# Moving LayerNorm's scale onto the first head's query weights, and the last 64 columns of a feed-forward product onto the moving side

## The chip, the cores and the metric

The kernel runs on one core of a Trainium2 chip. The metric is device time in microseconds (us), the median over several executions. Most executions agree within 0.3%, which is 4 us here. Figures read from a trace are of one execution each. Engines: PE is TensorE (PEld its weight loads), DVE is VectorE, ACT is ScalarE, POOL is GpSimd, SP is SyncE, which here only issues transfers.

## The reference, cut to what matters

```python
mod = (silu(c) @ w_mod).reshape(1, 6, 1, 640)          # c: 1 x 640, w_mod: 640 x 3840
sa, ca, ga, sb, cb, gb = ...                           # its six rows: shift, scale, gate, twice
h = layernorm(x) * (1 + ca) + sa                       # x: 2048 x 640
q = h @ wq                                             # 32 heads of 128
o = softmax(q @ k_cache.T / sqrt(128)) @ v_cache       # 2048 keys per head
x = x + ga * (o @ wo)
h = layernorm(x) * (1 + cb) + sb
x = x + gb * B(h)          # B ends with: gelu(layernorm(x1) @ w3) @ w4, w3: 640 x 1728
...
```

The attention of 32 heads makes up most of the time. The change touches what comes before the first scores, and the product with w3: 1728 = 13 x 128 + 64, so its last block of columns is half empty.

## The kernel before: the parts that are touched

The kernel records operations with a priority, and a list scheduler puts each engine's operations into a fixed order. Each engine then executes its own list strictly in that order.

The start: five loads of 128 rows of `w_mod` (scale and shift columns side by side, 2560 bytes a row), ten one-column products per load, then transposed rows are scaled and shifted as they leave PSUM.

```python
for k in range(KT):                                    # KT = 5
    wm_load.append(dma("ACT" if k % 2 else "SP", ... w_mod[k*128:(k+1)*128, 0:2*D], ...))
...
for k in range(KT):
    def mcol(e, k=k):
        for j in range(2 * KT):                        # shift columns, then scale columns
            ins = e.matmul(mc[:, j:j+1], wm_ap[:, k, j*128:(j+1)*128], s_bf[:, k:k+1], ...)
P.op("DVE", ... tensor_copy(saT.ap, mc[:, 0:KT]) ...)
P.op("DVE", ... tensor_scalar_add(out=caT.ap, in0=mc[:, KT:2*KT], scalar1=1.0) ...)
...
# chunk 0 of the rows: 4 tiles transposed on PE, then per k one pass on DVE or ACT
hT[0][k] = transposed * caT[:, k] + saT[:, k]
# first query: five products, each in two halves of 256 rows
e.matmul(mm[:, 0:z-a], wq_t[...], hT_t[ch][:, kk, a:z], ...)
```

The feed-forward part, per chunk of 512 rows (four chunks):

```python
for f in range(NF):                                    # NF = 14 blocks, the last padded to 128
    for kk in range(KT):
        e.matmul(m.ap, w3_ap[:, kk, f*128:(f+1)*128], nT_ap[ch][:, kk, :], ...)   # 512 columns
    e.activation(gT_ap[:, f, :], m.ap, GELU)
```

## Time and profile before

| | before |
|---|---|
| median of three runs | 1369.59 us (1368.27 to 1372.08) |
| profiled execution | 1368.34 us |
| last `w_mod` piece landed / first exponential started | 9.09 / 13.78 us |
| first exponential of steps 4 and 5 | 46.72 / 54.89 us |
| from there to the last exponential | 1137.78 us |
| from the last exponential to the end | 174.35 us |

A step is one head with one chunk of 512 rows. Its eight exponentials of 1024 columns are the only ACT operations of that size, so the time at which a step's first one starts is an easy landmark. The last three rows cut the span into start, middle and tail. The transfer view of the first 16 us gives the rate in 40 slices of 0.4 us:

```profile
GB/s 0 0 0 0 54 86 250 387 394 410 403 426 403 397 403 391 384 397 403 406 296 284 245 127 289 260 137 152 211 190 246 116 172 261 263 212 239 3 8 13
```

While `w_mod` streams in, the rate stays near 400 GB/s.

### The profile page before, as it was taken

Reading aid. Unit: us, or ns where it says so; the run is one execution under the profiler, and the core shown is the slowest. Engines: PE = TensorE matmul, PEld = TensorE weight load, DVE = VectorE, ACT = ScalarE, POOL = GpSimd, SP = SyncE. Lnnn points to the kernel's source line nnn. Section 1 sums busy time; section 2 is a strip of 40 time slices with the busy share of each in tenths; the row PEclk is TensorE's granted clock in tenths of the full one; section 3 lists DMA queues with packets and bytes.
Section 4 is the critical chain, followed back from the end, with each engine's and each line's share of the span. In section 5 each row is a group of like instructions: output and inputs, shape, how many; then the busy total and the mean of one; then the engine's idle time right before and its main releaser. Section 6 shows DMA issues by size and latency. Waiting matters only on the chain.

```text
span 1367.0 us, 29510 instructions
## 1 busy us (share of the span) xinstructions
PE 1348.4 (99%) x12778; PEld 934.7 (68%) x13012; DVE 574.7 (42%) x1442; ACT 1102.6 (81%) x1145; POOL 111.5 (8%) x97
## 2 busy tenths in 40 slices
PE   9999999999999999999999999999999999999999
PEld 5677677677667767767776766776776676655665
DVE  5554344544332332333233233233323345798553
ACT  6998888888888888888888888888888888833222
POOL 1000000000000000000000000000233337500000
PEclk9999999999999999999999999999999999999999
DMA  9742624172415221341305121522236000431110
GB/s 217 150 86 51 118 28 80 37 134 48 108 37 94 51 47 36 55 90 28 55 13 99 34 47 35 94 51 48 55 65 140 22 16 19 113 84 47 41 40 31
DMA packets 264932, 90.38 MB, mean 66 GB/s; under 512 B 245065, under 2 KB 262410, under 8 KB 264794
## 3 DMA queue, kind: packets, MB, share of 16 engines
q1 hardware_dynamic: 260826, 84.17, 30.5%
q0 software_dynamic: 672, 2.56, 0.8%
q8 instruction: 104, 1.70, 0.5%
q10 hardware_dynamic: 3296, 1.67, 0.5%
q14 instruction: 34, 0.28, 0.1%
HBM read 41.68 MB, written 2.63 MB: 32 GB/s over the span
## 4 chain that ended last, share of the span: by engine, by line
PE 97%; issue 1%; DMA 1%; DVE 1%; ACT 0%; SPq 0%; DVEq 0%
PE f_O L825 35%; PE f_S L806 29%; PE f_M L729 10%; PE f_M L760 10%; PE f_M L1008 2%; PE f_O L989 2%; PE f_S L989 2%; PE f_S L1008 2%; PE f_S L940 1%; PE f_S L963 1%; PE f_M L963 1%; PE f_O L940 1%; DMA f_W<-in_w_mod_dram 0%; DMA f_hT<-f_xn 0%; PE f_S L760 0%
## 5 line engine op out<-in xcount | busy, mean ns | idle before, releaser
L808 ACT ACTIVATE f_PQ<-f_S 128x1024 bf16<-128x1024 f32 x1024 | 1042.0, 1023 | 136.5 <-PE f_S L806 103.9
L825 PEld LDWEIGHTS f_O<-f_KV,f_PQ 128*128 128x128 bf16 x8192 | 634.9, 98 | 261.3 <-DVE f_OO L834 0.2
L825 PE MATMUL f_O<-f_KV,f_PQ 128*128 128x129 bf16 x8192 | 796.4, 220 | 8.3
L806 PE MATMUL f_S<-f_PQ,f_KV 128*128 128x512 bf16 x1831 | 650.8, 379 | 2.6 <-ACT f_PQ L808 0.5
L768 DVE TENSOR_TENSOR f_y<-f_M,f_y 128x320 f32<-128x320 f32 x192 | 94.4, 492 | 465.6 <-PE f_M L760 465.6
L760 PE MATMUL f_M<-f_wo,f_OO 128*128 128x320 bf16 x992 | 272.9, 299 | 0.0
L806 PEld LDWEIGHTS f_S<-f_PQ,f_KV 128*128 128x128 bf16 x2048 | 191.6, 98 | 13.3 <-ACT f_PQ L808 1.7
L729 PE MATMUL f_M<-f_hT,f_wq 128*128 128x512 bf16 (+1 forms) x635 | 189.1, 378 | 1.9 <-DVE f_tmp L771 0.2
L760 PEld LDWEIGHTS f_M<-f_wo,f_OO 128*128 128x128 bf16 x992 | 96.3, 98 | 28.5
L834 DVE TENSOR_TENSOR f_OO<-f_O,f_rl 128x256 bf16<-128x256 f32 x256 | 108.4, 423 | 8.3
L538 POOL TENSOR_TENSOR f_y<-f_y,f_mod 128x640 f32<-128x640 f32 x32 | 49.1, 1542 | 735.5 <-DVE f_y L768 735.4
L733 DVE CAST f_PQ<-f_M 128x512 bf16<-128x512 f32 x127 | 87.9, 692 | 49.9 <-PE f_M L729 49.6
L729 PEld LDWEIGHTS f_M<-f_hT,f_wq 128*128 128x128 bf16 x640 | 62.5, 98 | 50.6 <-DVE f_hT L595 0.8
L832 DVE RECIPROCAL f_rl<-f_O 128x2 f32<-128x2 f32 x256 | 43.6, 170 | 65.7 <-PE f_O L825 54.8
L992 ACT ACTIVATE f_OO<-f_S 128x512 bf16<-128x512 f32 x28 | 16.7, 597 | 43.6 <-PE f_S L989 43.6
L766 DVE COPY f_y<-f_M 128x320 f32<-128x320 f32 x32 | 15.7, 492 | 57.1 <-PE f_M L760 57.1
L499 DVE BATCH_NORM_STATS2 f_small<-f_y 128x6 f32<-128x320 f32 (+1 forms) x72 | 32.3, 481 | 2.5 <-DMA f_y<-in_A_x_dram 1.5
L1008 PE MATMUL f_M<-f_KV,f_OO 128*128 128x320 bf16 x224 | 31.7, 299 | 0.0
L1008 PE MATMUL f_S<-f_KV,f_OO 128*128 128x320 bf16 (+1 forms) x224 | 31.0, 296 | 0.0
L544 ACT ACTIVATE f_xn<-f_y,f_small 128x640 bf16<-128x640 f32 x10 | 9.1, 915 | 26.3 <-DVE f_small L523 21.2
L661 DVE TENSOR_REDUCE f_small<-f_tmp 128x1 f32<-128x640 f32 x20 | 16.4, 820 | 30.1 <-ACT f_PQ L808 30.1
L1008 PEld LDWEIGHTS f_M<-f_KV,f_OO 128*128 128x128 bf16 x224 | 21.9, 98 | 8.9
(151 smaller groups left out, 523.6 us busy)
## 6 DMA issues: line engine op xcount, KB each, us to landing
f_KV<-in_A_v_cache_dram SPq DMA_DIRECT2D x28, 512.0 KB, 5.0
f_wo<-in_A_wo_dram SPq DMA_DIRECT2D x8, 640.0 KB, 4.2
f_wq<-in_A_wq_dram SPq DMA_DIRECT2D x7, 640.0 KB, 4.5
f_xin<-in_A_x_dram SPq DMA_DIRECT2D x13, 320.0 KB, 3.4
out_dram<-f_xin SPq DMA_DIRECT2D x15, 160.0 KB, 1.8
f_KV<-in_B_w_dram SPq DMA_DIRECT2D x5, 432.0 KB, 3.8
f_KV<-in_A_k_cache_dram SPq DMA_TRANSPOSE x128, 2.8
f_OO<-f_OO SPq DMA_TRANSPOSE x128, 2.5
```

The source lines that it names most:

```text
L538: P.op(eng, lambda e: e.tensor_tensor(out=out, in0=a, in1=b, op=op), COST[eng][0], rd, wr, prio, lat=300 if eng == "POOL" else None, dual= ...
L729: P.op("PE", lambda e, i=i, kk=kk, mm=mm, a=a, z=z: e.matmul(mm[:, 0:z - a], wq_t[g % 2][:, kk, hh * 128:(hh + 1) * 128], hT_t[ch][:, kk, ...
L733: P.op("DVE", lambda e: e.tensor_copy(q.ap, m.ap), 690, (m,), (q,), s * NP - 90)
L760: P.op("PE", lambda e, m=m, qt=qt, hf=hf, hh=hh: e.matmul(m[:, 0:HD], OT_ap[gs][:, qt, hh, :], wo_t[g % 2][:, hh, hf * HD:(hf + 1) * HD], ...
L768: P.op("DVE", lambda e, m=m, yt=yt: e.tensor_tensor(out=yt.ap, in0=m[:, 0:HD], in1=yt.ap, op=ALU.add), 490, (m, yt), (yt,), s * NP - 60)
L806: P.op("PE", lambda e, sp=sp, r=r, kt=kt: e.matmul(sp[:, r * QC:(r + 1) * QC], K_ap[b][:, kt * 128:(kt + 1) * 128], q.ap, start=True, stop ...
L808: x = P.op("ACT", lambda e, sp=sp, pt=pt: e.activation(pt.ap.rearrange("p k q -> p (k q)"), sp.ap, ACT.Exp, scale=SCALE), 1021, (sp,), (pt ...
L825: ins = e.matmul(o[bk][:, w * 129:w * 129 + 129], pt[:, r, qt * 128:(qt + 1) * 128], V_ap[b][:, u, 0:129], start=(u == 0 and w == 0), stop ...
L832: P.op("DVE", lambda e, ov=ov, i0=i0: e.reciprocal(rl_t[:, i0:i0 + 2].unsqueeze(2), ov[:, 0:258].rearrange("p (u d) -> p u d", u=2)[:, :, ...
L834: evac.append(P.op("DVE", lambda e, ov=ov, i0=i0, bk=bk: e.tensor_tensor(out=On_ap[gs][:, 2 * bk:2 * bk + 2, hh, :], in0=ov[:, 0:258].rear ...
L989: P.op("PE", lambda e, m=m, f=f, kk=kk: e.matmul(m.ap, w3_ap[:, kk, f * 128:(f + 1) * 128], nT_ap[ch][:, kk, :], start=(kk == 0), stop=(kk ...
L1008: P.op("PE", lambda e, f=f, mm=mm, o=o, c0=c0, c1=c1: e.matmul(mm[:, o:o + c1 - c0], gT_ap[:, f, i * 128:(i + 1) * 128], w4_ap[f][:, c0:c1 ...
```

## The change

Intent: let the scores start sooner, and let PE do less in the half-empty w3 block. It has three parts.

**The start.** The first head's query weights are multiplied by the scale (five 128x128 operations on POOL) in place of the rows. The shift's share is one column for that head, added when q leaves PSUM. So the rows can be transposed and copied before any modulation is known. `w_mod` is loaded as ten pieces, the five scale halves first; K and V loads wait for the last pieces; the V loads and the next heads' query weights move from ACT's queue to SP's; the first of the four LayerNorm tiles moves to ACT.

**w3.** The 64 columns become the moving operand, with the rows as weights: twenty products of 64 columns in place of five of 512 per chunk.

**An ordering of POOL and DVE.** A POOL operation with two tensor inputs that the scheduler's model would start before, or up to 0.4 us after, the end of such a DVE operation waits for it.

```diff
+                if e == "DVE":
+                    last_dual = o
+                elif last_dual is not None and s < port["DVE"] + 400.0:
+                    o.deps.setdefault(last_dual, False)
...
-    for k in range(KT):
-        wm_load.append(dma(... w_mod[k * 128:(k + 1) * 128, 0:2 * D] ..., 320, ...))
+    load_wm(wms, D, -300)          # five loads of the scale half, 1280 bytes a row
+    load_wm(wmb, 0, -297)          # then five of the shift half
...
+            A_(... activation(xn[0].ap, x.ap, ACT.Copy, scale=-1.0 / D, accum_out=mu.ap) ...)
+            A_(... activation(xn[0].ap, x.ap, ACT.Square, bias=mu.ap, accum_out=ss.ap) ...)
...
+            for k in (0, 2, 1, 4, 3):
+                P.op("POOL", ... tensor_scalar(out=xn_t[4][:, k*128:(k+1)*128], in0=wq_t[0][:, k, 0:128],
+                                               scalar1=caT[:, k:k+1], ... op0=ALU.mult), 300, ...)
...
-    load_k(0, -297.5, gate=(wm[2],))
+    load_k(0, -296.5, gate=(wmb[4],))
...
+                    ins = e.matmul(bq_ps.ap, wq_t[0][:, kk, 0:128], b_bf[:, kk:kk + 1], ...)
+            x = P.op("DVE", ... tensor_scalar_add(out=q[:, 0:QC // 2], in0=m[:, 0:QC // 2], scalar1=bq.ap) ...)
...
+        for kk in range(KT):
+            for i in range(4):
+                ... e.matmul(m[:, c0:c0 + FL], nT_ap[ch][:, kk, i*128:(i+1)*128], w3_ap[:, kk, FN*128:FF], ...)
...
```

## The prediction

> **What bounds the kernel now.** I read the page first, then the chain of waits, then the timeline of the first 16 us and of the last 145 us, since the change touches only these two stretches (and, lightly, GpSimd's start times between them).
>
> ```profile
> span 1367.0 us, 29510 instructions
> ...
> PE 1348.4 (99%) x12778; PEld 934.7 (68%) x13012; DVE 574.7 (42%) x1442; ACT 1102.6 (81%) x1145; POOL 111.5 (8%) x97
> ...
> PE 97%; issue 1%; DMA 1%; DVE 1%; ACT 0%; SPq 0%; DVEq 0%
> ```
>
> PE is busy in 1348.4 of 1367.0 us, and 97% of the chain that ended last is PE. So there are two ways to gain: let PE do less, or let its real work start sooner. Work taken from DVE, ACT or POOL elsewhere is worth nothing. A busy PE is not all useful: before the attention starts it runs filler matmuls. The timeline of the start (columns: start us, us, then engine, line, operation, tiles) shows what the first useful work waits for:
>
> ```profile
> 4.73 1.68 PE L440 MATMUL f_S<-f_ones 128*128 128x512 bf16 x7
> ...
> 8.12 0.81 PEld L465 LDWEIGHTS f_M<-f_s_bf,f_W 128*128 128x128 bf16 x22
> ...
> 8.76 1.46 DVE L531 TENSOR_SCALAR f_xn<-f_xin,f_small 128x640 bf16<-128x640 bf16 x4
> ...
> 10.55 0.54 DVE L595 TENSOR_SCALAR f_hT<-f_O,f_small 128x512 bf16<-128x512 bf16 x1 [0.19 <-PE f_O L586]
> 10.60 0.78 ACT L590 ACTIVATE f_hT<-f_O,f_small 128x512 bf16<-128x512 bf16 x1 [1.29 <-PE f_O L586]
> ...
> 13.37 0.81 PE L806 MATMUL f_S<-f_PQ,f_KV 128*128 128x512 bf16 x3 [0.27 <-ACT f_PQ L737]
> 13.78 2.86 ACT L808 ACTIVATE f_PQ<-f_S 128x1024 bf16<-128x1024 f32 x3 [0.70 <-PE f_S L806]
> ```
>
> The scores start only at 13.37 us. The chain (start, us, what) gives the reason:
>
> ```profile
> 2.61 6.49 DMA f_W<-in_w_mod_dram
> 9.14 0.40 PE f_M L465 x10
> ...
> 10.55 1.01 DVE f_hT L595 x2
> ...
> 13.37 0.39 PE f_S L806
> ...
> 34.27 4.54 DMA f_hT<-f_xn
> 38.84 1.07 DVE f_hT L602 x3
> ```
>
> The last of five w_mod transfers lands at 9.10 us, then come its ten column products, the remaining transposes, the modulation of the rows (five passes on DVE and ACT), the query projection, its eviction. The last two lines matter for a rival: there is a second start-up wait at 38.8 us, for the second chunk's rows.
>
> In the tail, PE is full too (19.95 us of 20 from 1310 to 1330 us), and the w3 products run at an even pace, ACT idle between them:
>
> ```profile
> 1225.79 1.24 PE L989 MATMUL f_O<-f_wq,f_KV 128*128 128x512 bf16 x5
> ...
> 1226.87 1.24 PE L989 MATMUL f_S<-f_wq,f_KV 128*128 128x512 bf16 x5
> 1227.07 0.60 ACT L992 ACTIVATE f_OO<-f_O 128x512 bf16<-128x512 f32 x1 [0.48 <-PE f_O L989]
> ```
>
> Each group of five starts 1.08 us after the one before: 216 ns per matmul. There are 14 groups per chunk, 4 chunks, and the fourteenth is half zeros (1728 = 13 x 128 + 64).
>
> **What the Trainium skill says.** (1) "TensorE: Matmul & The Clock Gate", section "Wait — 56ns, not 53.3ns?": warm matmuls start N/2.4 + about 2.5 ns apart, and never closer than about 25 ns. The trace agrees: 216 ns at 512 columns. (2) The same page, "Back-to-back issue gap", says a stream of weight load and matmul pairs takes about 81 ns per pair at 128 columns. Here the trace disagrees: the chain shows twelve 129-column products in 0.68 us, 57 ns each with a weight load each, so the measurement decides. (3) "ScalarE: Activation LUTs", section "What ACT_TABLE_LOAD costs": an ACTIVATE with immediates takes 186 ns + 0.833 ns per element, each pointer operand adds about 93 ns; for 640 elements and two pointers that is 905 ns, and the trace has 915. (4) "DMA: Bandwidth & Descriptors", section "Anatomy of one DMA": about 2 us of a transfer is fixed. The smallest landing time of the row transposes here is 2.6 us, which fits with a little data time.
>
> **The change, part by part.**
>
> *w3's last block.* Per chunk, five 512-column matmuls (5 x 216 = 1.08 us) become twenty with 64 moving columns, one per token tile and k, with the rows as the stationary operand. By (1) the array time is 64/2.4 + 2.5 = 29 ns, but each has its own weight load. The closest thing in the trace is the one-column products of the start: 22 loads in 0.81 us, 37 ns each. At 129 columns the load is hidden under 57 ns. My estimate for 64 columns is 37 to 42 ns, so 20 x 40 = 0.80 us. Gain 0.28 us per chunk, 1.1 us for four (1.3 us at 37 ns). The GELU of this block halves (0.60 to about 0.4 us), on an engine that waits for PE anyway: 0. One extra row transpose per chunk (2.6 to 6 us to land) is issued first in the chunk and needed 13 groups = 14 us later: 0. The w4 products keep count and size: 224 + 224 + 14 of 128 rows, as the stacked half blocks still need one full-height product per tile. The DVE and POOL fills of the pads go or change place, off the path: 0.
>
> *The start.* Rows are transposed unmodulated; the first head's weight columns are scaled instead (five 128x128 operations on POOL), and the shift comes in as five one-column products whose result is added at the eviction of q. What this takes out from behind the last w_mod transfer: ten column products become five (0.2 us less); the twenty transposes, of which now most precede it; the modulating evictions (10.55 to about 12.05 us), now plain copies of halves that start as soon as the tiles are ready. What is left behind it is, in PE order: five column products 0.2, two fillers 0.43, five 256-column query products 0.55, five one-column products 0.19, five more query products 0.55, about 0.2 of latency, the eviction with bias about 0.45, 0.25 to the first scores: 2.8 us. Today it takes 13.37 - 9.10 = 4.27 us. The total bytes ahead are the same 1.6 MB of w_mod, now in ten pieces, with the K loads held back until the second half lands; I take 9.1 us as unchanged. The first scores then start at about 11.9 us, 1.45 us sooner. Check on DVE: today its four tiles' work ends at 10.22 us; one tile less saves two statistics, one aggregate and one normalisation, 2 x 0.42 + 0.12 + 0.36 = 1.3 us, so it ends near 9.0, the second halves are copied by about 10.7, and that just meets the PE order. ACT takes the first tile: two accumulating passes of about 0.75, three small ones of 0.2 and one of 0.91, about 3 us after its table load, done near 8 us. It fits.
>
> *What comes back.* K's pieces 1 to 3 of the first head wait for the last w_mod piece, behind one V and one wq load, so the first of them goes out near 10.0 us and lands 3.3 to 4.3 us later, 13.3 to 14.3. It is needed in slot 2, now 14.86, then 13.4 us. I charge 0.35 us. The second V half goes out near 14 us and is needed near 18.2 with 5.4 us typical landing: it too may cost; I put the two together at 0.5 us. Rows of chunk 0 are modulated after the first query on DVE, 5 x 0.4 us, before the second head's projection; DVE was idle 3.56 us there, so 0. The second chunk's rows (the wait at 38.8 us, some 0.7 us of PE idle time: score pairs 38.50 to 40.29 apart where the step before has 1.11) come earlier by some 1 us, not the full 1.45, since the transposing queue is busy without much slack: another 0.2. Net of the start: 1.45 - 0.7, about 0.8 us, 1.4 if none of this bites.
>
> *GpSimd's new waits for DVE's two-input operations.* POOL is busy 111.5 us and is not on the chain: 0.
>
> Sum: 1.1 + 0.8 = 1.9 us; upper end 1.3 + 1.4 = 2.7.
>
> **The rivals.** A: transfers take the place of the waits removed, so the start gains nothing (for: the DMA share is above 0.9 from 5 us on; the wait at 38.8 us ends at a transfer and absorbs any earlier start whose transfer does not move). Then only 1.1 us, 1368.1. B: the 64-column products pace like their weight loads and array time in series (37 + 29 = 66 ns): 1.3 us per chunk, a loss of 0.2 each, and with the full start gain the total is still 0 to -0.5 us: 1369. Against it: 57 ns at 129 columns shows that load and product overlap. C: everything lands, PE order meets no wait, and the products take 33 ns: 1.7 + 1.5, or a little more if the stall at 38.8 us also shrinks: 3.5 us, 1365.6. D: ACT becomes the start's bound, because its table load now comes after more transfer issues and the first tile's chain of six operations is serial; the first tile's transposes then hold PE's order up and the scores start near 12.7: half of the start's gain gone.
>
> **Range and chances.** The medians before are 1369.59 (1368.27 to 1372.08), and the profiled run took 1368.34, so the noise of a median is some 1 us and the true level perhaps 1369. From 1369 I take 2.2 us (between the sum of 1.9 and its upper end): 1366.8 us. Range 1364.6 to 1369.2: C with a fast draw, A or B with a slow one. A 2% change would be 27 us, more than the whole start and all w3 blocks affected together; the chance of either side is under 1%.
>
> **What will show it.** Right: first scores near 11.9 us, filler and column products before it; in the tail, a run of twenty 128x64 products of about 0.8 us at the head of each w3 chunk and the span from first w3 product to the end shorter by 1.1 us; PE's instruction count up by some 60 in that line. Wrong: first scores after 12.7 us, PE idle at slots 2 to 6 before a K or V transfer, a longer gap near 38 us, or twenty products in 1.08 us or more.

## More of the kernel before

The experiments fell on three chips, so versions are compared by their difference from the kernel before that ran beside them.

The busy time in two stretches (columns: stretch, its length, busy us and instruction count of PE, PEld, DVE, ACT, POOL, then PE's granted clock, the transfer share, GB/s):

```profile
10.00:15.00 5.00, 4.42 (x33) 2.16 (x32) 2.23 (x7) 3.05 (x5) 0.96 (x1) 1.00 1.55 197
...
44.00:49.00 5.00, 4.95 (x56) 3.58 (x55) 3.16 (x10) 4.74 (x5) 0.00 (x0) 1.00 0.07 24
```

The clock is full in both, and by 44 us PE has no gaps.

## The result, and the profile after

| | before | after |
|---|---|---|
| median (four runs each, same chip) | 1369.22 us (1368.27 to 1372.08) | 1370.39 us (1368.49 to 1372.13) |
| last `w_mod` piece landed | 9.09 us | 11.18 us |
| first exponential of step 0 | 13.78 us | 16.18 us |
| first exponential of steps 4 / 5 | 46.72 / 54.89 us | 53.48 / 61.65 us |
| from step 5 to the last exponential | 1137.78 us | 1137.50 us |
| from the last exponential to the end | 174.35 us | 171.66 us |

The ratio is 1.0005 (95% interval 0.9982 to 1.0028): the same at the 2% limit, but not the gain of 2 us that was predicted, and outside the range given. A ratio is the mean time of one kernel's fast runs over that of the other's of the same rounds, so it is not quite the ratio of the medians quoted here. The rows of the table already locate everything: the tail gained 2.7 us, the start lost 6.8 us in this execution (the profiled one, 1372.13 us, the slowest of the four).

The page of the changed kernel looks just like that of the kernel before:

```profile
span 1370.8 us, 29671 instructions
...
PE 1349.5 (98%) x12844; PEld 937.1 (68%) x13078; DVE 574.8 (42%) x1446; ACT 1105.4 (81%) x1155; POOL 114.8 (8%) x102
...
PE 97%; DMA 1%; issue 1%; ACT 1%; DVE 0%; SPq 0%; DVEq 0%
```

PE still makes 97% of the chain. Its busy time seems to have risen (1348.4 us before), but both traces lack 234 of PE's records; in the two repetitions of experiment 1, whose traces hold all of them, it fell from 1361.9 to 1360.3 us. Averages over the span hardly show this change; the stages do. The timeline of the start (start us, us, engine, line, operation, tiles; in brackets the idle time and what ended it):

```profile
9.38 0.16 DVE L488 TENSOR_SCALAR f_small<-f_M 128x5 f32<-128x5 f32 x1 [1.03 <-PE f_M L479]
...
9.96 3.06 POOL L643 TENSOR_SCALAR f_xn<-f_wq,f_small 128x128 bf16<-128x128 bf16 x5 [8.09 <-DMA f_wq<-in_A_wq_dram]
...
10.29 0.72 PE L479 MATMUL f_M<-f_s_bf,f_W 128*128 128x1 bf16 x15 [0.15 <-DMA f_W<-in_w_mod_dram]
10.38 0.43 DVE L548 TENSOR_SCALAR f_xn<-f_xin,f_small 128x640 bf16<-128x640 bf16 x1
...
12.99 1.27 PE L774 MATMUL f_M<-f_hT,f_xn 128*128 128x256 bf16 x5
...
15.77 0.81 PE L860 MATMUL f_S<-f_PQ,f_KV 128*128 128x512 bf16 x3 [0.36 <-ACT f_PQ L790]
16.18 2.85 ACT L862 ACTIVATE f_PQ<-f_S 128x1024 bf16<-128x1024 f32 x3 [0.70 <-PE f_S L860]
```

Four things are to be seen. The scale columns are ready at 9.5 us, ahead of the shift columns. The five weight scalings on POOL take 3.06 us and can start only when the weights have landed. PE waits for shift columns that land later than all of `w_mod` did before. And the last LayerNorm tile is normalised only at 10.38 us. The chain of waits (start, us, what) holds the second loss:

```profile
3.56 6.68 DMA f_W<-in_w_mod_dram
...
36.87 7.04 DMA f_hT<-f_xn
...
45.05 0.61 PE f_M L774
```

The wait for the second chunk's rows, which ended at 38.8 us before, ends at 43.9 us now. Transfer rate and clock of the same stretches as before:

```profile
GB/s 0 0 0 0 32 125 250 394 387 390 378 349 320 263 221 317 330 373 339 311 304 338 350 325 254 134 57 20 1 172 156 45 137 205 271 252 86 133 99 179
```

```profile
10.00:15.00 5.00, 4.81 (x56) 3.56 (x54) 2.42 (x11) 1.32 (x4) 4.01 (x6) 0.66 0.68 130
...
44.00:49.00 5.00, 4.24 (x20) 2.06 (x22) 3.59 (x11) 1.26 (x2) 0.00 (x0) 0.66 0.87 274
```

The rate sags between 4.4 and 6.4 us, down to 221 GB/s, and the granted clock is 0.66 in both stretches: in each there is a window of 3.41 us at half clock (from 10.92 and from 45.05 us). The Trainium skill, "TensorE: Matmul & The Clock Gate", section "What's actually happening", says that PE runs at half clock after an idle window of about 3.4 us (3413 ns) and that the windows are not tied to the program. The trace agrees in length and in factor, but the stretches before were not idle: PE was busy for 2.54 of the 3.42 us before the first window and for 1.28 of the 3.41 us before the second. The halving explains part of why the same kernel's executions differ: of the nine of the changed kernel, the three with a mean clock of 0.998 or 0.999 took 1370.9 to 1372.1 us, and of the six at full clock five took 1368.0 to 1370.0 us and one 1371.88. The kernel before has such executions too, only fewer (of the 17 on experiment 1's chip, one at 0.998 took 1371.33 us and one at 0.999 took 1373.15).

In the tail, the new products (the timeline again, of the first chunk's w3 part):

```profile
1231.19 0.75 PE L1044 MATMUL f_O<-f_KV,f_wq 128*128 128x64 bf16 x20
1231.99 2.10 PE L1052 MATMUL f_S<-f_wq,f_KV 128*128 128x512 bf16 x9
```

A trap lies here. The next group begins 0.80 us after these twenty, which would be exactly the predicted time. But in the trace's records the twenty start 29 ns apart, 19 x 29 = 0.55 us from first to last, and the next recorded start comes 0.246 us after the last. That is 29 + 217 ns: the record of one 512-column product is missing (the trace holds 63 of the 65 products of this part). So twenty take 20 x 29 = 0.58 us. The repetition's trace (`a1_again` below), which holds all records, shows it directly:

```profile
1228.04 0.75 PE L1044 MATMUL f_O<-f_KV,f_wq 128*128 128x64 bf16 x20
1228.62 2.32 PE L1052 MATMUL f_S<-f_wq,f_KV 128*128 128x512 bf16 x10
```

A check that needs no single record: from the last exponential to the start of the last w4 block is 155.76 us before and 153.77 after, 1.99 us less, which is four times 1.08 - 0.58. The tail as a whole is 2.7 us shorter; the other 0.7 us lies behind that point and is not explained (in the other versions with the w3 part the tail is 171.6 to 172.3 us).

### The profile page after: what moved, and what is told of

It is laid out like the page before. It is cut to its first block, busy times and chain, and to the rows that moved or that the text cites. A ratio compares the mean times of both kernels' runs of the same rounds, so it can differ in the third digit from the quotient of the medians.

```text
span 1370.8 us, 29671 instructions
## 1 busy us (share of the span) xinstructions
PE 1349.5 (98%) x12844; PEld 937.1 (68%) x13078; DVE 574.8 (42%) x1446; ACT 1105.4 (81%) x1155; POOL 114.8 (8%) x102
## 4 chain that ended last, share of the span: by engine, by line
PE 97%; DMA 1%; issue 1%; ACT 1%; DVE 0%; SPq 0%; DVEq 0%
PE f_O L879 35%; PE f_S L860 29%; PE f_M L774 10%; PE f_M L814 10%; PE f_M L1071 2%; PE f_S L1071 2%; PE f_S L1052 2%; PE f_O L1052 2%; PE f_S L1016 1%; PE f_S L993 1%; PE f_O L993 1%; PE f_M L1016 1%; DMA f_hT<-f_xn 1%; DMA f_W<-in_w_mod_dram 0%; ACT f_PQ L862 0%
## 5 line engine op out<-in xcount | busy, mean ns | idle before, releaser
L774 PE MATMUL f_M<-f_hT,f_wq 128*128 128x512 bf16 x630 | 188.5, 380 | 3.9 <-DVE f_hT L578 2.0
L1071 PEld LDWEIGHTS f_S<-f_KV,f_OO 128*128 128x128 bf16 x224 | 21.7, 98 | 8.2
```

The costliest lines, as they stand in the source:

```text
L774: P.op("PE", lambda e, i=i, kk=kk, mm=mm, a=a, z=z, w=w: e.matmul(mm[:, 0:z - a], w, hT_t[ch][:, kk, a:z], start=(i == 0), stop=(i == KT - ...
L1071: P.op("PE", lambda e, f=f, mm=mm, o=o, c0=c0, c1=c1: e.matmul(mm[:, o:o + c1 - c0], gT_ap[:, f, (i % 2 if f == FN else i) * 128:][:, 0:12 ...
```

## The experiments

**Theory.** The w3 part gains 2 us, and the start loses more than that, for four separable reasons: the smaller pieces of `w_mod` move slower; POOL's scaling sits on the path; K's held-back loads push the transposing queue, and with it the second chunk's rows; and the order within DVE and PE. **Rivals.** The w3 part does not gain and the difference is merely noise; or one cause (the clock halving, or shift columns behind the last piece) makes up the whole loss; or the POOL-DVE ordering costs time.

### 1. Both kernels again

No edit. Repetitions of the changed kernel (first) and of the kernel before (second).

> The changed kernel once more. Theory (the start loses what the w3 blocks gain): the profile again has its first exp after 14.5 us (16.18 before this run, 13.78 in the kernel before), and from the last exp to the end it is about 2 us shorter than the kernel before (171.7 against 174.4). Rival (the one profile caught a bad draw of the transfers, the start is neutral): first exp at 13.5 us or sooner and the median about 2 us below the kernel before.

> The kernel before against itself, for the noise: ratio 1.000 within 0.002. Theory: first exp within 0.5 us of 13.78 and step 5's first exp within 1 us of 54.89. Rival (the start's transfers differ this much from run to run): either of them off by 2 us or more.

Measured: 1370.04 us (1367.99 to 1371.65), ratio 1.0005 [0.9992, 1.0018]; and 1368.53 us, ratio 0.9998. So the changed kernel is some 1.2 us slower or equal, certainly not 2 us faster. Its new trace, at full clock from 6.8 us on, where the record of the clock begins, still starts at 16.05 us, and step 5 at 58.50 us; the kernel before has 14.19 and 55.37 us in its new trace, within what was expected of it.

A second way to count helps from here on. Counted from the landing of the last `w_mod` piece, the first exponential follows after 4.63 to 4.78 us in all six traces with the old start, after 5.00 us in the profiled execution of the changed kernel, part of which ran at half clock, and after 4.00 us in this repetition (16.05 - 12.05). So the path behind the landing did become shorter, by 0.7 us; the landing, 3.0 us later than in the kernel before's first trace, makes up more than the whole loss at the first exponential here. Timeline lines of the repetition:

```profile
10.84 2.99 POOL L643 TENSOR_SCALAR f_xn<-f_wq,f_small 128x128 bf16<-128x128 bf16 x5 [8.97 <-DMA f_wq<-in_A_wq_dram]
...
13.89 0.28 PE L774 MATMUL f_M<-f_hT,f_xn 128*128 128x256 bf16 x1 [0.22 <-POOL f_xn L643]
...
17.79 0.59 PE L860 MATMUL f_S<-f_PQ,f_KV 128*128 128x512 bf16 x2 [0.91 <-DMA f_KV<-in_A_k_cache_dram]
```

The fifth query product waits for POOL, and the scores of the second slot wait 0.91 us for a K piece. Both waits are there without any clock halving, so the halving cannot be the whole cause.

### 2. The parts alone: w3, the start, the ordering

w3 alone is the kernel before with the w3 and w4 edits only; the start alone is the changed kernel with these undone (it keeps the ordering).

```diff
 # w3 alone: before.py
+        m = Tile(pool="T")
+        for kk in range(KT):
+            for i in range(4):
+                ... 128x64 products ...
-        for f in range(NF):
+        for f in range(FN):
 ...
 # start alone: the changed kernel with this reversed
```

> The kernel before with only the w3 and w4 part of the change (last block as twenty 64-column products, layout, pads). Theory: the start is that of the kernel before (first exp 13.8 us), each 20 products take 0.6 us, not 1.08, so the time is 1.9 us less, ratio 0.9986. Rival (the w3 part gains nothing in the end, the 2 us seen in the trace are jitter of the last transfers): ratio 1.000, last exp to end 174 us.

> The kernel before with all of the change but its w3 and w4 part. Theory: first exp 14.5 to 16.5 us, step 5's first exp 2 to 7 us later than before's 54.89, the time 2 to 5 us longer, ratio 1.002 to 1.0035. Rival (start neutral or a gain as predicted): first exp under 13.5 us, ratio 0.999 to 1.000.

Measured: w3 alone 1367.31 us (1366.88 to 1367.92), ratio 0.9985 [0.9972, 0.9998]; start alone 1372.95 us (1372.55 to 1376.79), ratio 1.0031 [1.0017, 1.0046]. One part gains and the other loses, and the intervals of both exclude 1. But w3 alone is not as good as its tail promises: its tail is 172.00 us (174.35 before), while its middle is 1138.81 us, 1.03 us longer than before, although no operation of the middle changed. Its trace shows where, in the second to last step:

```profile
1175.91 1.55 POOL L542 TENSOR_TENSOR f_hT<-f_tmp,f_y 128x640 bf16<-128x640 f32 x1
...
1176.24 3.39 DVE L865 SCALAR_TENSOR_TENSOR f_y<-f_hT,f_small,f_mod 128x640 f32<-128x640 bf16 x1
...
1177.42 1.53 POOL L542 TENSOR_TENSOR f_y<-f_y,f_mod 128x640 f32<-128x640 f32 x1
...
1180.09 1.25 PE L733 MATMUL f_M<-f_hT,f_wq 128*128 128x512 bf16 x5 [0.89 <-DVE f_tmp L775]
```

A DVE operation with two tensor inputs that elsewhere takes 0.87 us took 3.39 us: it lay under two POOL operations with two inputs each, ended 0.68 us after the second of them, and PE waited 0.89 us for what came behind it on DVE. (In the kernel before the same operation took 1.88 us: the collision was there in a mild form.) The Trainium skill, "GPSIMD Engine Reference", section "Specifications", says that POOL's memory interfaces are shared with DVE and that DVE instructions with two inputs contend; this trace agrees, with a factor of nearly 4. So the ordering, which the prediction put at 0, was tried: once with w3, once alone.

```diff
 # w3 and ordering: w3 alone, and
+                if e == "DVE":
+                    last_dual = o
+                elif last_dual is not None and s < port["DVE"] + 400.0:
+                    o.deps.setdefault(last_dual, False)
 # ordering alone: before.py with these lines only
```

> The kernel before with the w3 and w4 part and the part that keeps GpSimd's shared-port operations behind DVE's, that is the change without anything of its start. The last attention step took 10.2 us with the w3 part alone, 9.1 in both the kernel before and the changed one. Theory G (the GpSimd part removes this 1.1 us): the last step takes 9.1 us, the time is 1366.1 us, ratio 0.9977. Rival (the 1.1 us are an accident of the order, GpSimd's part does nothing): 1367.2, ratio 0.9985.

> The version with the w3 part and GpSimd's waits and the old start, once more on this chip beside the other two: 1365.5 to 1366.8 us again, ratio 0.9975 to 0.9985; if the earlier gain was the luck of one chip, 1367 or more.

> The kernel before with GpSimd's new waits for VectorE's two-input operations alone. Theory 1 (the waits only repair a collision in the last attention step that the w3 part brings, as that step took 9.14 us in the kernel before already): same as the kernel before within 0.5 us, 1368.3 to 1369.2. Theory 2 (the two engines hold each other up elsewhere too): 1366.9 to 1367.8, about 1.3 us faster, with the difference spread over several steps of the attention. My prediction's figure of 0 holds under theory 1.

Measured: w3 and ordering 1365.96 us (1365.40 to 1366.57), ratio 0.9978 [0.9965, 0.9992], and again 1366.31 us, ratio 0.9980 [0.9967, 0.9994]. Ordering alone 1368.73 us, ratio 0.9997. In the trace of the two together:

```profile
1176.77 0.87 DVE L871 SCALAR_TENSOR_TENSOR f_y<-f_hT,f_small,f_mod 128x640 f32<-128x640 bf16 x1
...
1177.72 1.54 POOL L548 TENSOR_TENSOR f_hT<-f_tmp,f_y 128x640 bf16<-128x640 f32 x1 [1.23 <-DVE f_y L871]
```

POOL now waits 1.23 us for DVE, DVE is done in 0.87 us, and the middle is 1137.50 us. The ordering has almost no gain of its own (0.23 us of the middle's length, nothing in the median); it repairs a collision that the w3 part's shifted schedule makes worse, and is worth about 1 us with it: 1.30 us of the middle in the traces (1138.80 - 1137.50), and 0.8 to 1.2 us of the medians (-1.6 us for w3 alone, -2.4 and -2.8 us with the ordering, each against the kernel before of its own chip). This is the first of two places where two parts of the change cannot be added up singly. The version with w3 and the ordering, on the old start, beats both kernels.

The sums close: start part +4.0 us (1372.95 - 1368.92), w3 with ordering -2.4 and -2.8 us (against 1368.67 and 1368.76), together +1.2 to +1.6; the changed kernel's repetition measured +1.1.

### 3. Whole rows of `w_mod`

```diff
-    load_wm(wms, D, -300)
-    load_wm(wmb, 0, -297)
+    for k in range(KT):
+        dma(... w_mod[k * 128:(k + 1) * 128, 0:2 * D] ..., 320, (), (wms[k], wmb[k]), -300 + 0.1 * k)
```

> The changed kernel with w_mod loaded again in five pieces of whole 2560-byte rows, everything else as changed. Theory R (ten pieces of 1280-byte rows move at 220 to 350 GB/s where the five moved at 390 to 410, so the last shift half lands at 11.2 to 12.1 us, not 9.1): the last w_mod piece lands at 9.6 us or sooner, and the first exp comes 0.5 to 1.5 us sooner, at 14.6 to 15.6, as the first head's weights then land at about 9.8 and POOL still needs 3.0 us. Rival (the transfers are slowed by the mixing with the 256-byte rows of wq or by other load at this time): the last piece lands after 10.5 us as in the changed kernel.

Measured: 1368.91 us (1366.94 to 1370.74), ratio 0.9999; first exponential at 15.24 us. The rate, in the same slices as before:

```profile
GB/s 0 0 0 0 38 109 208 384 391 406 400 407 413 410 390 384 378 384 403 410 324 279 258 226 215 121 182 266 222 214 92 149 125 18 195 110 127 136 26 129
```

The sag is gone, and the last piece lands at 9.09 us instead of 11.18. So the sag is due to the split into ten half-row pieces. Whether it is the row length, the number of pieces or their order is not shown; the row length alone does not do it, since the rows of x, also 1280 bytes long, moved at 379 GB/s from 3.0 to 3.5 us in the kernel before. The late landing has a second part that the rival names: the first head's query weights, issued at 3.1 us in both versions, stand in the changed kernel ahead of three of the shift pieces in SP's queue, and here behind all of `w_mod`. `w_mod` and both query-weight loads together had landed by 11.75 us in the changed kernel and by 10.45 us here. By that estimate the slower transfer makes up some 1.3 of the 2.1 us and the order in the queue the other 0.8; no edit separated them. What the pieces were meant to buy, an early scale, they did not bring: in the changed kernel the last scale piece lands at 9.02 us, when in this version everything is there. The first exponential is 0.8 to 0.9 us earlier, not the 2.1 us of the landing: another wait ends last now, that of the fifth query product for POOL's scaling (10.01 to 13.02 us).

### 4. The scaling on DVE

```diff
-                P.op("POOL", lambda e, k=k: e.tensor_scalar(... scalar1=caT[:, k:k + 1] ...), 300, (wq[0][0], caT), (wp[k],), -280)
+                P.op("DVE", lambda e, k=k: e.tensor_scalar(... scalar1=caT[:, k:k + 1] ...), 150, (wq[0][0], caT), (wp[k],), -276)
```

> The changed kernel with the five weight scalings on DVE instead of POOL. Theory P (the five POOL operations take 3.0 us from the landing of the weights, and the last query product waits for them; I had left this out): five DVE operations of about 0.15 us each, the query products of the first half without a wait for POOL, first exp about 0.5 us sooner (15.5), time 0 to 1 us less. Rival (the wait for the shift columns in PE's order is what ends last, POOL is hidden): first exp unchanged within 0.2 us.

Measured: 1370.52 us (1369.06 to 1371.17), ratio 1.0010 [0.9996, 1.0023]; first exponential at 14.96 us. Timeline lines:

```profile
10.01 0.91 DVE L643 TENSOR_SCALAR f_xn<-f_wq,f_small 128x128 bf16<-128x128 bf16 x5 [0.36 <-DMA f_wq<-in_A_wq_dram]
...
18.60 1.01 PE L860 MATMUL f_S<-f_PQ,f_KV 128*128 128x512 bf16 x2 [2.82 <-DMA f_KV<-in_A_k_cache_dram]
```

The five take 0.91 us on DVE and 3.06 on POOL, and the first exponential is 1.1 to 1.2 us earlier. Most of that is not the edit's: experiment 5's repetition, with the scaling on POOL, also starts at 14.96 us. Counted from the landing of the last `w_mod` piece, it is 3.65 us here against 4.00 and 3.98 us in the two traces at full clock with the scaling on POOL, so the edit is worth some 0.3 us there. The median does not move. In this trace the time turns into another wait: PE stands 2.82 us before K's second piece, and step 1 starts at 27.09 us (24.13 in the changed kernel). The piece was issued at 12.28 us, as late as in the changed kernel (12.15), but landed at 18.47 us instead of 16.71, and the clock was halved from 18.53 us for 3.41 us. So that K's late issue takes the gain is a reading of one unlucky trace and not shown; if it holds, it is the second place where single parts cannot be added up. In a version with this edit, whole rows and K gated as before (experiment 7), step 1 starts at 22.53 us.

### 5. K earlier

```diff
-    load_k(0, -296.5, gate=(wmb[4],))
+    load_k(0, -296.5, gate=(wms[4],))                  # K after the last scale piece
-        dma("SP", ... A_v_cache ..., 256, (wmb[4],), (t,), -295.6 if a == 0 else -293.5)
+        dma("ACT", ... A_v_cache ..., 256, (), (t,), -296.5, after=(ln0[3],))
...
```

> The changed kernel with the first head's K loads released by the scale columns, not the shift columns, and the first V halves on the other queue again. Theory K (holding K back makes PE wait for K's second piece in slot 2 and moves the whole queue of transposes, with the second chunk's rows in it, later): no PE wait for K in the first step, step 1's first exp within 8.0 us of the first one (8.6 in the second run of the changed kernel), step 4's first exp about 1 to 2 us sooner against 50.33. But K's packets then compete with the shift columns, so the first exp may be up to 0.7 us later. Rival (K is no bottleneck): step 4 minus step 0 stays at 34.3 us or more.

> The kernel with K released early once more, for a profile in a draw whose clock is not halved (its first profile fell on the one slow execution of five, 1373.1 at 0.998). Theory K: first exp 15.5 to 16.5, step 4's first exp at 49 or sooner, no PE wait for K in step 0; median again 1367 to 1368. Rival: the four good executions were luck, median 1369 or more.

Measured: 1367.25 us (1367.07 to 1367.70, and the profiled one of 1373.12 at clock 0.998), ratio 0.9990 [0.9976, 1.0003]; again 1367.59 us, ratio 0.9997. In the repetition's trace step 4 starts at 48.40 us, while the changed kernel's two traces have 53.48 and 50.33. Of that, part is the start's landing, which came 1.1 us earlier in this trace than in the second of the two; from step 0 to step 4 it took 33.44 us against 34.28. No other single edit of the start gained as much in the median: 2.3 to 2.5 us against the changed kernel's repetition, each counted from its own kernel before. The edit also returns V to ACT's queue, and the two are not separated. Of the expectations, step 1 within 8.0 us of the first exponential held in the first trace (7.96) and not in the second (8.92); step 4 minus step 0 gave the rival's sign in the first, half-clocked one (36.83 us). The one slow execution started late (17.39 us) and had two windows of half clock again, so the clock risk stays.

### 6. More fillers, to keep the clock up

```diff
-    mcols(wms, D, mcs, ..., 1)
-    mcols(wmb, 0, mcb, ..., 0)
+    mcols(wms, D, mcs, ..., 3)
+    mcols(wmb, 0, mcb, ..., 1)
```

> The changed kernel with more filler matmuls between the column products (3 instead of 1 behind each scale product, 1 instead of 0 behind each shift product). Theory C (in about half of its executions the PE clock is halved from 10.9 us for 3.4 us because PE idles between the column products, and these are the executions of 1371 us and more): the granted clock stays at 1.0 in the start, no execution over 1370, median 1368.5, first exp still near 16 us. Rival (the slow draws come from the transfers, not the clock): the times stay in two groups, 1368 and 1371.

Measured: 1372.52 us (1370.70 to 1373.10), ratio 1.0023 [1.0010, 1.0037], the slowest variant but the start alone. The halving at 10.9 us did not occur, but the one behind the wait for the second chunk's rows did (at 46.38 us, 3.41 us long), and the fillers stand in PE's order ahead of work. Three of the five executions had a mean clock of 0.999, so the expectation missed. In the traces a halving follows a stretch in which PE waits; filling one wait does not help while the other is there.

### 7. The three together, and what is left

First all three mends at once: whole rows, scaling on DVE, K gated as before. Then two attempts on the order. The first, on the changed kernel with DVE scaling and early K, moves the shift columns' products behind the first half of the query. The second is the first of these versions with the scale columns' DVE operation behind all normalisations, and with a tile of its own for the last row tile's deviation.

```diff
 # the order of the shift products
-    mcols(wmb, 0, mcb, [-282 + 0.1 * k for k in range(KT)], 0)
+    mcols(wmb, 0, mcb, [-265.9 + 0.01 * k for k in range(KT)], 0)
 # the order on DVE
-    P.op("DVE", ... tensor_scalar_add(out=caT.ap, ...), 170, (mcs,), (caT,), -290)
+    P.op("DVE", ... tensor_scalar_add(out=caT.ap, ...), 170, (mcs,), (caT,), -280.5, slack=1500.0)
-                    rstd_act(gs[1], 3, 4, prio - 90)
+                    rstd_act(gs[1], 3, 4, prio - 90, rs=rs_l)
...
```

> The changed kernel with three of its start's parts undone at once: w_mod in whole rows, the scalings on DVE, K released by the first and third w_mod pieces and V on the other queue, as before. The algebra (scaled weights, shift at the query, first tile on ACT) is kept. Theory (each of R, P and K takes its part and what is left is the intended gain): first exp at 13.0 to 14.0 us, step 5's first exp at or under 55, clock at 1.0, time 1365 to 1367, ratio 0.997 to 0.999. Rival (the algebra itself costs, through PE's order and the second modulation): first exp still over 14.5 us, time no better than the kernel before with the w3 part, 1367.3.

> The changed kernel with scale columns still loaded first in ten pieces, the scalings on DVE, K released by the scale columns, and the shift products moved in PE's order behind the first half of the query products. Theory (PE's order puts the shift products, whose columns land last, ahead of the transposes of tiles 3 and 4; with them behind, the early scale columns are worth something): transposes of tiles 3 and 4 no later than 10.6 us, first exp 13.7 to 14.7 us. Rival (the slow 1280-byte rows and the late landing of the first head's weights end last anyway): first exp 14.9 or later, as in the run with DVE scalings.

> The whole-row, DVE-scaling, early-K version of the changed kernel, with two edits on VectorE's order: the operation that forms the scale columns is placed behind all three normalisations, and the fourth tile gets a reciprocal-deviation tile of its own, so that its ScalarE operations no longer wait for the third tile's normalisation. If the order (a wait for the scale columns in front of the third and fourth normalisation) is what is left of the start's loss: the three normalisations run back to back and end by 9.9 to 10.0 us (11.09 without the edit), the fourth tile's transposes start by 10.1 to 10.4 us (11.14), and the first exponential moves from 14.58 us to 13.8 to 14.2 us; it can hardly fall below 13.7, because VectorE must still do copies (1.5 us), scaling (0.9), and evictions (0.65) behind them. Median 1366.5 to 1367.5 us. Rival (the chain from the last w_mod piece over scaling, query and shift products sets the time, and the order does not matter): tile 4 is early but the first exponential stays at 14.4 us or later, 1367.5 to 1368.3.

Measured: all three 1367.89 us (1366.29 to 1369.69), ratio 0.9995, first exponential at 14.58 us, step 5 at 55.87: all three outside what was expected, and with the rival's signs. The order of the shift products 1368.89 us, ratio 0.9998, first exponential at 16.10 us: a miss, since the last tile was normalised only at 11.26 us there. The order on DVE 1367.88 us (1365.74 to 1370.01), ratio 0.9989 [0.9975, 1.0002].

With all three mends the first exponential is still 0.4 to 0.8 us later than in the kernel before's two traces, with `w_mod` there at 9.03 us (9.09 and 9.55). Its timeline:

```profile
9.39 0.16 DVE L488 TENSOR_SCALAR f_small<-f_M 128x5 f32<-128x5 f32 x1 [0.46 <-PE f_M L479]
...
9.94 0.20 ACT L521 ACTIVATE f_small<-f_small 128x1 f32<-128x1 f32 x1 [1.49 <-DVE f_xn L548]
...
10.64 0.45 DVE L548 TENSOR_SCALAR f_xn<-f_xin,f_small 128x640 bf16<-128x640 bf16 x1
```

In DVE's order the scale columns stand ahead of the third tile's normalisation, so DVE waits for `w_mod`; ACT's step for the fourth tile waits for the third normalisation, because both use one tile of deviations; so the fourth tile is normalised at 10.64 us. The order edit removes this:

```profile
8.41 1.16 DVE L548 TENSOR_SCALAR f_xn<-f_xin,f_small 128x640 bf16<-128x640 bf16 x3 [0.58 <-ACT f_small L522]
...
10.31 0.72 PE L631 MATMUL f_O<-f_ident,f_xn 128*128 128x128 bf16 x10
```

All three normalisations are done by 9.57 us. Yet the first exponential came at 15.15 us, so by the figures the rival held: the order of DVE was not what sets the time. The landing has to be taken out of that, though. In that execution the last piece landed at 9.91 us instead of 9.03. Counted from the landing, the first exponential follows after 5.24 us (5.55 without the edit, 4.69 before). So DVE's order was worth some 0.3 us (from one trace each), not the 0.4 to 0.8 that I had expected. What follows in the trace is the rest. The first ten transposes start at 10.31 us, although their tiles have long been ready: PE's order puts them behind the scale columns' products, which wait for `w_mod`. And behind them DVE is nearly fully busy from 11.07 to 14.05 us with copies, scalings and the query's eviction. That these two make up the remaining 0.55 us is read from one trace and was not tested by a further edit.

The first steps also vary by themselves: in the version with the order edit, step 1 to 2 took 10.86 us in the profiled execution (8.17 normally), with waits of 1.1 us for a K transfer and 1.2 us for DVE, and its five runs spread over 4.3 us. The w3 version with ordering, on the old start, spreads over 1.6 us at most. But the kernel before, with the same old start, spread over 5.4 us in its repetition (1367.75 to 1373.15), so the spread is not the new start's alone.

## Why the prediction was wrong, point by point

1. **"20 x 40 = 0.80 us" for the new products.** Right in mechanism, mis-sized. They start 29 ns apart, the array time that the prediction itself had worked out; the weight load is hidden even at 64 columns. The term is 0.50 us per chunk, 2.0 us in all, instead of 1.1. My 37 ns came from one-column products, which are no model for this.
2. **"POOL is busy 111.5 us and is not on the chain: 0."** This step failed. An engine off the chain slowed another here: DVE's operation took 3.39 us in place of 0.87. Without the ordering the w3 part would have given back about 1 us. In the kernel before there was next to nothing to repair: the ordering alone measured 1368.73 against 1368.67 us. So 0 was right for the ordering alone, and wrong for the change it came with.
3. **"The total bytes ahead are the same ... I take 9.1 us as unchanged."** This step failed, and it is the first of the start's loss: 11.18 and 12.05 us in two executions. The rate fell to between 213 and 350 GB/s, and the bytes ahead were not the same: a load of query weights now lay before the last shift pieces. Whole rows, ahead of those weights again, brought 9.09 back.
4. **"What is left behind it is, in PE order ...: 2.8 us."** The direction was right: at full clock the first exponential followed the landing after 4.00 us in place of 4.69. But that is 0.7 us saved and not the 1.45 us that the sum gave. The list left out the scaling of the weights (3.06 us on POOL, behind a weight transfer that landed just before 10 us) as a thing to wait for. Counted from the landing, that was worth some 0.3 us (one trace); the rest of the difference stays open.
5. **"So it ends near 9.0"** for DVE's four-tile work. It ended at 10.81 us (10.38 + 0.43), since the sum of durations said nothing of the wait for the scale columns in the middle of DVE's list.
6. **"I put the two together at 0.5 us"** for K and V, and **"another 0.2"** for the second chunk's rows. For K and V the direction was right and the size too small; for the rows even the sign was wrong, since they were forecast some 1 us earlier and came 3.6 to 5.1 us later. K's first piece went out at 10.26 us (6.98 before), and the second chunk's rows came at 43.91 and 42.42 us instead of 38.81; that the one pushed the other through the transposing queue is the likely reading, not tested apart. Step 3 to 4 took 12.32 us in one execution, 8.93 in another, 8.65 before. K earlier alone (with V back on its old queue) gave 2.3 to 2.5 us of the total back.
7. **Not foreseen at all**: the clock. After stretches in which PE waited for late transfers, its clock was halved for 3.41 us in some executions, more often than in the kernel before.

The figure that came nearest was that of rival A (a transfer takes the place of the wait removed), 1368.1 us. Its mechanism was the right one, but it took the start's gain for zero at worst; that the figure came near is partly luck, since two errors in the w3 part's favour (points 1 and 2) offset part of the start's loss. The prediction of "faster by over 2%" and its opposite as under 1% each held. The range failed because every rival assumed that the start cannot become slower than it was.

## What to carry to other kernels

Before taking work off a path that waits for a transfer, count what the new path waits for, engine by engine in program order, and ask whether the transfers themselves get a new row length or a new place in the queue: several separate losses at the start, from some tenths of a us to a few us, made a well-aimed change worthless. An operation list summed by durations is not a finishing time; look for the first operation in that list that waits for something else. Count from the landing of the transfer as well as from zero, or a lucky or unlucky landing passes for the effect of an edit. And test the parts of a change singly and together: here the part that cost nothing to write (two engines kept from running two-input operations at the same time) was worth a third to a half of the best version's gain.

## What the Trainium skill lacked or had wrong

- "TensorE: Matmul & The Clock Gate", "Back-to-back issue gap", gives about 81 ns per pair at 128 columns and about 131 ns at 512. Here pairs at 64 columns start 29 ns apart, at 129 columns 57 ns and at 512 columns 216 ns, each with its own weight load. The formula in the section "Wait — 56ns, not 53.3ns?" fits all three.
- "GPSIMD Engine Reference", "Engine selection", calls one-input operations on POOL roughly line-rate. Five 128x128 bf16 scalings by a per-partition column took 3.06 us on POOL (0.61 us each) and 0.91 us on DVE. No run here separates a fixed part per operation from the rate.
- "DMA: Bandwidth & Descriptors", "Specifications", has 512 bytes as the least for full rate. The changed kernel's loads of 1280-byte rows ran at 387 to 394 GB/s between 2.8 and 4.0 us and then sagged to 221; with 2560-byte rows in their place the rate stayed between 378 and 413. The page does not foresee the sag, and the runs do not tell whether row length, number or order of the pieces makes it.
